# The scaled second copy of the first batch's query and key upper parts, made by ScalarE in place of VectorE

## The chip, the cores and the metric

One core of one Trainium2 chip runs the whole program. The metric is device time in microseconds (us) for one execution, and the quoted time before is the median of three runs. Engines are named as in the profile: PE is TensorE's matmul, PEld its weight load, DVE is VectorE, ACT is ScalarE, POOL is GpSimd, SP is the engine whose queue issues most transfers.

## What is computed

Three layers follow each other. The first is attention with a hash mask, over 2 batches, 8 heads, 768 positions and 64 columns; the second a gated feed-forward layer; the third a routed layer with 8 experts of which each token uses two.

```python
q_bucket = bits_to_int(einsum('bhsd,dk->bhsk', q, proj) > 0)      # the same for k
scores = where(q_bucket == k_bucket, (q @ k.T) / sqrt(64), -1e9)
x = softmax(scores) @ v                                           # 1536 x 512 after a transpose
h = x @ w_in                                                      # 512 x 2048
x = (h * sigmoid(1.702 * h)) @ w_out                              # 2048 x 512
logits = x @ w_gate + log1p(exp(x @ w_noise)) * noise             # top 2 of 8 experts per token
out[token] += weight * (relu(x @ w1[e]) @ w2[e])                  # w1[e]: 512 x 1024
```

## The kernel before

Every float32 operand of an exact matmul is split into two float16 tiles, an upper part and the rest. For a query tile (two heads, two of the six 128-row groups, so 128x256 elements) or a key tile (one head, all six groups, 128x384 elements) the function `stack_hi` does the first half of that: line L144 rounds the loaded tile to its upper part (DVE in the first batch), line L145 subtracts it from the tile on POOL, and L149 or L151 writes a second copy of the upper part, scaled by 1/32, into the tile that TensorE will read beside the rest. Which engine makes that copy is read from a table of four letters, `SC`: first batch's queries, second batch's queries, first batch's keys, second batch's keys; A is ScalarE (L149), D is VectorE (L151). In the first batch there are 12 query tiles and 8 key tiles.

`stack_lo` (L158, ACT) then writes the scaled rest into the same tile `qsa` or `ks`, and SP issues a transposing transfer of it (L169). From the transposed tile TensorE computes the hash bits (`buckets`, L179 and L180), ACT copies them out (L184), DVE makes a bucket number and a one-hot row of it (`one_hot`, L189 to L203), ACT scales it (L210), and a second transposing transfer (L211) brings it to the place from which `qk` (L254) computes masked scores. `qsa` has one buffer, `qsb` (the upper parts and one-hots of a query tile) two.

The 96 score tiles of 128 rows are numbered g = 0 to 95, 48 for each batch. For each of them DVE takes the row maximum out of PSUM (`rowmax`, L266), ACT the exponential (L275), and TensorE transposes the result (L293, with ACT copies L301) or, from the 17th tile on, it is split again (L314, L321, L323) and transposed by a transfer (L327). `pv` multiplies with the values. There are two PSUM buffers for scores, so `qk` for tile g+2 waits until `rowmax` has read tile g.

Between these steps the 32 blocks of the feed-forward weights are loaded as 64-bit words and converted: SP issues the load into a ring of three `wraw` buffers (L417), DVE turns the bits into float32 (L428, L431, L434), ACT or POOL scales (L444, L442), ACT makes the upper part (L445) and POOL the rest (L446), which frees the buffer. The feed-forward matmuls of the first 256 rows (L460, L471, with `th` on DVE in L490) begin when tile 16 and the first blocks are through.

The program names a step g for each piece of work. Up to step 99, which holds all attention work and nearly all feed-forward work, the framework's scheduler puts the instructions of each engine in order from its own estimate of their times; from step 100 the order is the written one. Each engine runs its row in order, so an instruction that waits holds all that stand behind it.

Of the kernel before, what the change touches and what calls it, by code (L numbers as in the profile page):

```python
# [53 lines left out]


PARAM = dict(GM=16, HE=lambda nm, b: 'D', OE=lambda nm, b: 'D', SC=lambda nm, b: 'D', WB=0, XO=lambda b: 'D', NG=16, WS=lambda i: 'P', TS=lambda g: True, XL=lambda g: 'D', GW=2, E0=7, T0=12, T1=16, EL=8, WX=3, PV={(1,2,3):4}, PVD=5, ST={}, VA={}, RA={}, O0=48, OS=2, IS=2, FU=16, VF=2, EC=lambda g: 'AA', QX=8, QS=3, EA=1, S1=(8,8,8,9,9,9,11,13), QE=8, XG=2, XB=2, PC=2, OH=3, BK=3, R0=18, R1=0, LK=8, WL=1, NW=3, LE=lambda nc: nc.scalar, I0=24, LQ=8, LV=0, W=[(g, 1) for g in range(-6, 30)], KA={(0,0,0):-8,(0,0,1):-6,(0,1,0):-4,(0,1,1):-2}, QA={(0,0,0):-7,(0,0,1):-3}, HI=lambda g: 'P', LO=lambda g: False)
PARAM.update(KA={(0, 0, 0): -15, (0, 0, 1): -6, (0, 1, 0): -5, (0, 1, 1): -4, (0, 2, 0): -1, (0, 2, 1): 1, (0, 3, 0): 4, (0, 3, 1): 5, (1, 0, 0): 37, (1, 0, 1): 39, (1, 1, 0): 44, (1, 1, 1): 46, (1, 2, 0): 42, (1, 2, 1): 51, (1, 3, 0): 47, (1, 3, 1): 51}, QA={(0, 0, 0): -15, (0, 0, 1): -3, (0, 0, 2): 1, (0, 0, 3): 3, (0, 1, 0): 8, (0, 1, 1): 9, (0, 1, 2): 17, (0, 1, 3): 21, (0, 2, 0): 24, (0, 2, 1): 28, (0, 2, 2): 30, (0, 2, 3): 33, (1, 0, 0): 37, (1, 0, 1): 41, (1, 0, 2): 47, (1, 0, 3): 52, (1, 1, 0): 57, (1, 1, 1): 56, (1, 1, 2): 60, (1, 1, 3): 69, (1, 2, 0): 72, (1, 2, 1): 69, (1, 2, 2): 80, (1, 2, 3): 84}, VA={(0, 0, 0): -1, (0, 0, 1): -3, (0, 1, 0): -1, (0, 1, 1): -1, (0, 2, 0): 0, (0, 2, 1): 0, (0, 3, 0): -1, (0, 3, 1): -2, (1, 0, 0): -1, (1, 0, 1): -1, (1, 1, 0): 2, (1, 1, 1): -4, (1, 2, 0): -3, (1, 2, 1): -3, (1, 3, 0): 2, (1, 3, 1): -2}, PV={(0, 0, 0): 4, (0, 0, 1): 5, (0, 0, 2): 6, (0, 0, 3): 5, (0, 1, 0): 6, (0, 1, 1): 4, (0, 1, 2): 4, (0, 1, 3): 5, (0, 2, 0): 5, (0, 2, 1): 5, (0, 2, 2): 5, (0, 2, 3): 6, (1, 0, 0): 4, (1, 0, 1): 5, (1, 0, 2): 4, (1, 0, 3): 5, (1, 1, 0): 5, (1, 1, 1): 5, (1, 1, 2): 5, (1, 1, 3): 6, (1, 2, 0): 6, (1, 2, 1): 4, (1, 2, 2): 4, (1, 2, 3): 4}, RA={0: 18, 1: 18, 2: 19, 3: 24, 4: 18}, W=[(g,1) for g in [-6, -4, -3, -1, 0, 0, 1, 1, 2, 4, 4, 7, 8, 8, 9, 10, 11, 12, 13, 14, 15, 16, 16, 17, 18, 20, 20, 22, 22, 23, 23, 24]], EC=lambda g:'AA', LE=lambda nc:nc.sync, HI=lambda g:'AAAA'[g%4], LO=lambda g:[0, 0, 0, 1, 0, 0, 0, 1][g%8]==1, S1=[8, 8, 8, 8, 8, 11, 13, 22], ST={0: 4, 1: 4, 2: 5, 3: 4, 4: 5, 5: 3}, NG=28, WS=lambda i:'PAAA'[i%4], HE=lambda nm,b:'DPDD'[2*(nm=='k')+b], OE=lambda nm,b:'DTDD'[2*(nm=='k')+b], SC=lambda nm,b:'DADD'[2*(nm=='k')+b], R1=2, I0=26, IS=1, O0=56, OS=1, GM=100, BK=3, OH=3, QX=8, QS=2, QE=7, VF=0, T0=12, T1=17, EL=10, WX=5, WL=2, PC=2, GW=2, E0=8, WB=2)
# [1094 lines left out]
```

## Time and profile before

| quantity | value |
|---|---|
| median of 3 runs | 826.06 us (823.59 to 827.40) |
| the profiled execution's own time | 823.72 us |
| its span from first to last instruction | 822.0 us |
| TensorE busy over the span | 715.9 us (87%) |
| VectorE busy | 533.9 us (65%) |
| ScalarE busy | 445.0 us (54%) |
| GpSimd busy | 267.9 us (33%) |
| mean granted TensorE clock | 0.96 |

The shares are means over a program with different stages, so a share of 65% can hide a stretch in which an engine never rests. The profiled execution took 1.72 us beside its span, and lies 2.34 us below the median.

### The profile page before, as it was taken

How to read it: one execution, taken by the hardware profiler on the slowest of the kernel's cores; microseconds unless marked ns; L12 is line 12 of the kernel's file. 1: busy time of each engine (PE TensorE's matmuls, PEld its weight loads, DVE VectorE, ACT ScalarE, POOL GpSimd, SP SyncE). 2: the span in 40 equal slices, each digit the busy share in tenths (PEclk: the TensorE clock that was granted, in tenths of full speed). 3: DMA queues.
4: the chain of work that ended last, by engine and by line, in shares of the span. 5: the costliest groups of instructions: out<-in, count | busy, mean ns of one | idle time of the engine just before them, and what ended most of it. 6: DMA issues, size and time to landing. Idle time of an engine off the chain costs nothing.

```text
span 822.0 us, 14816 instructions
## 1 busy us (share of the span) xinstructions
PE 715.9 (87%) x5398; PEld 446.0 (54%) x5399; DVE 533.9 (65%) x1330; ACT 445.0 (54%) x859; POOL 267.9 (33%) x303
## 2 busy tenths in 40 slices
...
GB/s 218 224 251 212 180 187 184 255 277 218 175 171 195 154 200 192 225 159 106 119 176 123 102 156 88 221 146 180 250 158 173 199 111 232 135 194 176 28 19 47
DMA packets 268126, 140.04 MB, mean 170 GB/s; under 512 B 224720, under 2 KB 243856, under 8 KB 268048
## 3 DMA queue, kind: packets, MB, share of 16 engines
...
## 4 chain that ended last, share of the span: by engine, by line
PE 42%; DVE 5%; DMA 3%; POOL 2%; issue 1%; ACT 1%; POOLq 0%; ACTq 0%; DVEq 0%
PE ph L799 15%; PE py L821 13%; PE px L471 6%; PE h L460 3%; PE py L825 2%; DVE er L323 1%; DMA xg<-slots 1%; PE pv L368 1%; POOL slots L685 1%; DMA slots<-xr,si 1%; DMA et<-er 1%; PE s L254 1%; ACT er L314 1%; DVE e L266 1%; DVE th L490 1%
## 5 line engine op out<-in xcount | busy, mean ns | idle before, releaser
L460 PE MATMUL h<-xt,wi 128*128 128x256 f16 x1152 | 140.2, 277 | 6.2 <-DVE mx L279 3.2
L799 PE MATMUL ph<-xg,ew 128*128 128x400 f16 (+2 forms) x864 | 135.4, 320 | 8.9 <-DMA xg<-slots 8.4
L743 DVE SCALAR_TENSOR_TENSOR ew<-w,ew 128x1024 f16<-128x1024 f32 x64 | 77.9, 1226 | 88.2 <-ACT ew L742 88.0
L471 PE MATMUL px<-wo,gt 128*128 128x512 f16 x576 | 132.6, 382 | 0.5 <-DVE th L490 0.4
L460 PEld LDWEIGHTS <-wi 128*128 128x128 f16 x1152 | 112.5, 99 | 28.2 <-issue 9.1
L821 PE MATMUL py<-ew,ht 128*128 128x512 f16 x576 | 125.8, 379 | 0.0
...
L254 PE MATMUL s<-kt,qt 128*128 128x512 f16 (+1 forms) x384 | 88.2, 353 | 33.3 <-DVE mx L266 28.5
L799 PEld LDWEIGHTS <-ew 128*128 128x128 f16 x864 | 82.6, 100 | 59.8 <-issue 6.8
L275 ACT ACTIVATE e<-e,mx 128x768 f32<-128x768 f32 x96 | 89.4, 931 | 27.9 <-DVE mx L266 21.5
L505 POOL TENSOR_TENSOR gt<-th,gt 128x512 f16<-128x512 f32 x48 | 60.1, 1252 | 122.0 <-ACT gt L504 121.6
L266 DVE CUSTOM_DVE_ANT_0 e<-s,zero 128x768 f32<-128x768 f32 x96 | 90.6, 948 | 4.4 <-PE s L254 1.5
L821 PEld LDWEIGHTS <-ht 128*128 128x128 f16 x576 | 56.3, 98 | 67.0
L471 PEld LDWEIGHTS <-gt 128*128 128x128 f16 x576 | 55.3, 98 | 64.1 <-issue 3.2
L323 DVE SCALAR_TENSOR_TENSOR er<-e,mx,er 128x768 f16<-128x768 f32 x68 | 73.1, 1080 | 25.9 <-ACT er L314 25.3
L314 ACT ACTIVATE er<-e,mx 128x768 f16<-128x768 f32 x68 | 63.0, 930 | 37.8 <-DMA et<-er 21.6
L835 ACT ACTIVATE yo<-py,wv 128x512 f32<-128x512 f32 (+1 forms) x32 | 20.3, 633 | 102.4 <-PE py L821 54.6
L809 ACT ACTIVATE ht<-ph 128x400 f16<-128x400 f32 (+2 forms) x72 | 33.5, 466 | 73.0 <-PE ph L799 72.9
L254 PEld LDWEIGHTS <-qt 128*128 128x128 f16 x384 | 37.0, 103 | 62.7 <-issue 38.5
L810 DVE SCALAR_TENSOR_TENSOR ht<-ph,ht 128x400 f16<-128x400 f32 (+2 forms) x72 | 37.6, 524 | 49.5 <-ACT ht L809 49.5
L742 ACT ACTIVATE ew<-w 128x1024 f16<-128x1024 f32 x64 | 66.3, 1047 | 2.6 <-DMA w<-in_moe_w_dram 2.6
L368 PE MATMUL pv<-et,vt 128*64 128x256 f16 x720 | 51.2, 284 | 7.5 <-DMA et<-er 7.5
...
## 6 DMA issues: line engine op xcount, KB each, us to landing
...
```

Source lines behind the costliest of these rows:

```text
L254: nc.tensor.matmul(ps[:, n0 * 128:n1 * 128], qt[:, s, h, t, :], kt[:, s, h, n0:n1, :].rearrange("p c t -> p (c t)"), start=(s == 0), stop= ...
L266: nc.vector.tensor_tensor_reduce(e32, st[g]["ps"][:, :S], zero.to_broadcast([128, S]), -0.125, TOP, op0=OP.add, op1=OP.min, accum_out=mx[: ...
L275: nc.scalar.activation(e32, e32, AF.Exp, scale=-1.0, bias=st[g]["mx"][:, 1:2], accum_out=sms[b, cc, hp][:, 2 * h + t:2 * h + t + 1] if g < ...
L314: nc.scalar.activation(er[:, 0], st[g]["e"], AF.Copy, scale=r)
L323: nc.vector.scalar_tensor_tensor(er[:, 1], d["e"], d["mx"][:, 3:4], er[:, 0], op0=OP.mult, op1=OP.subtract)
L460: nc.tensor.matmul(ph[:, a, :], wi[ws][:, d, f0:f0 + 128], xt[:, d, xs, :], start=(d == 0 and ws == 0 and xs == 0), stop=(d == HP - 1 and ...
L471: nc.tensor.matmul(px, gts[ci, f // 2][:, gs, f % 2, t * 128:t * 128 + 128], wo[ws][:, f, :], start=(f == 0 and gs == 0 and ws == 0), stop ...
L505: nc.gpsimd.tensor_tensor(gt[:, 1], th, gt[:, 0], op=OP.subtract)
L742: nc.scalar.activation(hi, x, AF.Copy, scale=SW1 if j == 0 else SW2)
L743: nc.vector.scalar_tensor_tensor(lo, x, SW1 if j == 0 else SW2, hi, op0=OP.mult, op1=OP.subtract)
L799: nc.tensor.matmul(ph[:, :c1 - c0], w[:, ws, d * FE + f * 128:d * FE + f * 128 + 128], xg[e, p][:, xs * HP + d, :], start=(d == 0 and ws = ...
L821: nc.tensor.matmul(py, ht[:, f, hs, t * 128:t * 128 + 128], w[:, ws, f * DM:(f + 1) * DM], start=(i == 0), stop=(i == n - 1))
```

## The change

Two of the four letters of `SC` become A: those of the first batch's queries and of the first batch's keys. The 12 + 8 copies of L151 in the first batch are then made by `nc.scalar.activation` in L149. Nothing else in the program text differs.

```diff
 PARAM.update(
 ...
-SC=lambda nm,b:'DADD'[2*(nm=='k')+b],
+SC=lambda nm,b:'AAAD'[2*(nm=='k')+b],
 ...
 )
```

Since the scheduler orders the instructions again, they also stand elsewhere. The first piece is DVE's row at the start of the program, where `k_131` and `q_133` are the first key and query tile as loaded and `p` is the projection:

```order
 L144 TENSOR_SCALAR ks<-k_131 128x6x64
 L144 TENSOR_SCALAR qsb<-q_133 128x4x64
-L151 TENSOR_SCALAR ks<-ks 128x6x64
-L151 TENSOR_SCALAR qsa<-qsb 128x4x64
 L97 TENSOR_SCALAR p_138<-p_135 128x6
 L98 TENSOR_TENSOR p_135<-p_135,p_138 128x6
```

DVE goes from the upper parts straight to the projection. The second piece is ACT's row at the same place:

```order
-L158 ACT_TABLE_LOAD
+L149 ACT_TABLE_LOAD
+L149 ACTIVATE ks<-ks 128x6x64
+L149 ACTIVATE qsa<-qsb 128x4x64
 L158 ACTIVATE ks<-k_131 128x6x64
 L158 ACTIVATE qsa<-q_133 128x4x64
+L149 ACTIVATE ks<-ks 128x6x64 x2
 L184 ACTIVATE pc<-pb 128x72
```

Both new copies stand ahead of both L158 rows that the first transposing transfers wait for. The third piece is DVE's row in the middle of the first batch, where `wraw_789` is the 15th of the 32 weight blocks and `e32_948` the 12th row maximum. Before:

```order
L428 TENSOR_SCALAR wf_869<-wraw_739 128x512
L194 TENSOR_REDUCE bk_1024<-pc_991 128x4
L266 ISA e32_948,mx_947<-s_880,zero_85 128x768
L266 ISA mx_947 128x1
L431 SCALAR_TENSOR_TENSOR wf_869<-wraw_739,wf_869 128x512
L203 TENSOR_TENSOR qsb_864<-iota_i_78,bk_1024 128x4x64
L434 SCALAR_TENSOR_TENSOR wraw_739<-wraw_739,wf_869 128x512
L266 ISA e32_994,mx_993<-s_942,zero_85 128x768
L266 ISA mx_993 128x1
L428 TENSOR_SCALAR wf_937<-wraw_789 128x512
L338 TENSOR_SCALAR sm_785<-sm_785 128x4
L431 SCALAR_TENSOR_TENSOR wf_937<-wraw_789,wf_937 128x512
```

And with the change:

```order
L431 SCALAR_TENSOR_TENSOR wf_869<-wraw_739,wf_869 128x512
L189 TENSOR_TENSOR pc_991<-pc_991 128x4x6
L434 SCALAR_TENSOR_TENSOR wraw_739<-wraw_739,wf_869 128x512
L191 TENSOR_TENSOR pc_991<-pc_991,pow2_89 128x4x6
L194 TENSOR_REDUCE bk_1024<-pc_991 128x4
L428 TENSOR_SCALAR wf_937<-wraw_789 128x512
L203 TENSOR_TENSOR qsb_864<-iota_i_78,bk_1024 128x4x64
L431 SCALAR_TENSOR_TENSOR wf_937<-wraw_789,wf_937 128x512
L434 SCALAR_TENSOR_TENSOR wraw_789<-wraw_789,wf_937 128x512
L266 ISA e32_948,mx_947<-s_880,zero_85 128x768
L266 ISA mx_947 128x1
```

The 15th weight block's three instructions, of which the first stood behind the 13th row maximum (`e32_994`), now stand ahead of the 12th. At the 13th row maximum DVE's row has passed two more weight blocks than before, at the 18th one more, and from the 33rd on the order of row maxima and weight blocks is the old one.

## Rows read from the trace of the kernel before

**Rows 1.** The page, parts 1 and 4: busy time by engine, the chain that ended last.
```profile
PE 715.9 (87%) x5398; PEld 446.0 (54%) x5399; DVE 533.9 (65%) x1330; ACT 445.0 (54%) x859; POOL 267.9 (33%) x303
PE 42%; DVE 5%; DMA 3%; POOL 2%; issue 1%; ACT 1%; POOLq 0%; ACTq 0%; DVEq 0%
```

**Rows 2.** Windows, stretch from:to and its length, then PE, PEld, DVE, ACT, POOL busy.
```profile
0.00:70.00 70.00, 37.18 (x302) 23.16 (x303) 65.73 (x167) 45.08 (x108) 37.06 (x73) 0.85 0.98 232
70.00:100.00 30.00, 16.14 (x110) 9.64 (x109) 22.33 (x48) 23.04 (x55) 16.81 (x17) 0.89 0.74 183
100.00:175.00 75.00, 61.19 (x495) 40.79 (x495) 72.54 (x136) 55.17 (x105) 41.73 (x35) 0.91 0.94 218
175.00:470.00 295.00, 267.77 (x2297) 179.48 (x2297) 232.72 (x667) 193.47 (x392) 94.90 (x88) 0.98 0.91 170
470.00:822.00 352.00, 333.63 (x2202) 192.94 (x2198) 140.55 (x315) 128.21 (x202) 77.44 (x92) 0.98 0.59 148
```

**Rows 3.** Waits of PE, 0 to 175 us: total us, times, longest.
```profile
PE s L254 <- DVE mx L266: 24.2, 16, 4.0
PE pb L179 <- DVE ks L144: 9.0, 1, 9.0
PE pb L179 <- DMA kt<-ks: 7.2, 3, 4.2
PE pv L352 <- DVE r L342: 6.3, 4, 3.5
PE pb L179 <- DMA qt<-qsa: 6.0, 3, 2.6
PE pb L179 <- ACT pc L184: 3.0, 1, 3.0
```

**Rows 4.** Windows of line L151 alone: DVE busy and count.
```profile
0.00:70.00 70.00, 7.22 (x14) 0.85 0.98 232
70.00:100.00 30.00, 0.91 (x2) 0.89 0.74 183
100.00:175.00 75.00, 1.62 (x3) 0.91 0.94 218
```

**Rows 5.** Line L151: duration ns, min/median/max (8 of the key rows are the second batch's).
```profile
L151 DVE TENSOR_SCALAR ks<-ks x16: 246/350/1118, 4.0 to 274.6; 128x384 f16<-128x384 f16 x16
L151 DVE TENSOR_SCALAR qsa<-qsb x12: 213/228/1177, 4.9 to 193.9; 128x256 f16<-128x256 f16 x12
```

**Rows 6.** Timeline of DVE and of POOL, 112.7 to 114.2 us: start, us, instruction.
```profile
113.00 1.18 DVE L151 TENSOR_SCALAR qsa<-qsb 128x256 f16<-128x256 f16 x1
114.10 0.94 DVE L266 CUSTOM_DVE_ANT_0 e<-s,zero 128x768 f32<-128x768 f32 x1
...
112.72 1.37 POOL L446 TENSOR_TENSOR wo<-wraw,wo 128x512 f16<-128x512 f32 x1 [1.06 <-ACT wo L445]
```

**Rows 7.** Line L149 on ACT (second batch) and line L210 on ACT, groups.
```profile
L149 ACT ACTIVATE qsa<-qsb x12: 398/416/418, 208.7 to 400.3; 128x256 f16<-128x256 f16 x12
...
L210 ACT ACTIVATE ks<-ks 128x384 f16<-128x384 f16 x8 | 4.2, 519 | 3.5 <-DVE ks L203 3.5
```

**Rows 8.** Timeline at the start, ACT and SP.
```profile
4.87 0.52 ACT L158 ACTIVATE ks<-k 128x384 f16<-128x384 f32 x1
...
5.41 1.33 SPq L169 DMA_TRANSPOSE kt<-ks  x1
```

**Rows 9.** Timeline of DVE: where the weight conversion waits for its load.
```profile
82.22 0.45 DVE L428 TENSOR_SCALAR wf<-wraw 128x512 int32<-128x512 int32 x1 [2.35 <-DMA wraw<-in_moe_w_in_dram]
90.68 0.43 DVE L428 TENSOR_SCALAR wf<-wraw 128x512 int32<-128x512 int32 x1 [2.77 <-DMA wraw<-in_moe_w_out_dram]
95.59 0.92 DVE L428 TENSOR_SCALAR wf<-wraw 128x512 int32<-128x512 int32 x1 [1.34 <-DMA wraw<-in_moe_w_out_dram]
```

**Rows 10.** Timeline of SP: first and last of five weight loads issued one after another.
```profile
86.78 0.33 SPq L417 DMA_DIRECT2D wraw<-in_moe_w_out_dram  x1
...
104.37 0.33 SPq L417 DMA_DIRECT2D wraw<-in_moe_w_out_dram  x1
```

More of the change, by code (lines that the diff above doesn't have):

```diff
@@ L56 @@
 PARAM = dict(GM=16, HE=lambda nm, b: 'D', OE=lambda nm, b: 'D', SC=lambda nm, b: 'D', WB=0, XO=lambda b: 'D', NG=16, WS=lambda i: 'P', TS=lambda g: True, XL=lambda g: 'D', GW=2, E0=7, T0=12, T1=16, EL=8, WX=3, PV={(1,2,3):4}, PVD=5, ST={}, VA={}, RA={}, O0=48, OS=2, IS=2, FU=16, VF=2, EC=lambda g: 'AA', QX=8, QS=3, EA=1, S1=(8,8,8,9,9,9,11,13), QE=8, XG=2, XB=2, PC=2, OH=3, BK=3, R0=18, R1=0, LK=8, WL=1, NW=3, LE=lambda nc: nc.scalar, I0=24, LQ=8, LV=0, W=[(g, 1) for g in range(-6, 30)], KA={(0,0,0):-8,(0,0,1):-6,(0,1,0):-4,(0,1,1):-2}, QA={(0,0,0):-7,(0,0,1):-3}, HI=lambda g: 'P', LO=lambda g: False)
-PARAM.update(KA={(0, 0, 0): -15, (0, 0, 1): -6, (0, 1, 0): -5, (0, 1, 1): -4, (0, 2, 0): -1, (0, 2, 1): 1, (0, 3, 0): 4, (0, 3, 1): 5, (1, 0, 0): 37, (1, 0, 1): 39, (1, 1, 0): 44, (1, 1, 1): 46, (1, 2, 0): 42, (1, 2, 1): 51, (1, 3, 0): 47, (1, 3, 1): 51}, QA={(0, 0, 0): -15, (0, 0, 1): -3, (0, 0, 2): 1, (0, 0, 3): 3, (0, 1, 0): 8, (0, 1, 1): 9, (0, 1, 2): 17, (0, 1, 3): 21, (0, 2, 0): 24, (0, 2, 1): 28, (0, 2, 2): 30, (0, 2, 3): 33, (1, 0, 0): 37, (1, 0, 1): 41, (1, 0, 2): 47, (1, 0, 3): 52, (1, 1, 0): 57, (1, 1, 1): 56, (1, 1, 2): 60, (1, 1, 3): 69, (1, 2, 0): 72, (1, 2, 1): 69, (1, 2, 2): 80, (1, 2, 3): 84}, VA={(0, 0, 0): -1, (0, 0, 1): -3, (0, 1, 0): -1, (0, 1, 1): -1, (0, 2, 0): 0, (0, 2, 1): 0, (0, 3, 0): -1, (0, 3, 1): -2, (1, 0, 0): -1, (1, 0, 1): -1, (1, 1, 0): 2, (1, 1, 1): -4, (1, 2, 0): -3, (1, 2, 1): -3, (1, 3, 0): 2, (1, 3, 1): -2}, PV={(0, 0, 0): 4, (0, 0, 1): 5, (0, 0, 2): 6, (0, 0, 3): 5, (0, 1, 0): 6, (0, 1, 1): 4, (0, 1, 2): 4, (0, 1, 3): 5, (0, 2, 0): 5, (0, 2, 1): 5, (0, 2, 2): 5, (0, 2, 3): 6, (1, 0, 0): 4, (1, 0, 1): 5, (1, 0, 2): 4, (1, 0, 3): 5, (1, 1, 0): 5, (1, 1, 1): 5, (1, 1, 2): 5, (1, 1, 3): 6, (1, 2, 0): 6, (1, 2, 1): 4, (1, 2, 2): 4, (1, 2, 3): 4}, RA={0: 18, 1: 18, 2: 19, 3: 24, 4: 18}, W=[(g,1) for g in [-6, -4, -3, -1, 0, 0, 1, 1, 2, 4, 4, 7, 8, 8, 9, 10, 11, 12, 13, 14, 15, 16, 16, 17, 18, 20, 20, 22, 22, 23, 23, 24]], EC=lambda g:'AA', LE=lambda nc:nc.sync, HI=lambda g:'AAAA'[g%4], LO=lambda g:[0, 0, 0, 1, 0, 0, 0, 1][g%8]==1, S1=[8, 8, 8, 8, 8, 11, 13, 22], ST={0: 4, 1: 4, 2: 5, 3: 4, 4: 5, 5: 3}, NG=28, WS=lambda i:'PAAA'[i%4], HE=lambda nm,b:'DPDD'[2*(nm=='k')+b], OE=lambda nm,b:'DTDD'[2*(nm=='k')+b], SC=lambda nm,b:'DADD'[2*(nm=='k')+b], R1=2, I0=26, IS=1, O0=56, OS=1, GM=100, BK=3, OH=3, QX=8, QS=2, QE=7, VF=0, T0=12, T1=17, EL=10, WX=5, WL=2, PC=2, GW=2, E0=8, WB=2)
```

1 line of the change is left out of this document (added).

## The prediction

> **What bounds the kernel now.** I read the page's busy shares and the chain of waits first. TensorE is busy 87% of the span and holds 42 of the hundredths that the chain names, VectorE 5 [rows 1]; so most of the program is a row of matmuls, and nothing that is done to VectorE there can pay. The change, however, touches only copies that run in the first 194 us [rows 5], so the mean shares say little and I cut the span into stretches [rows 2]. What to see: from 175 us on TensorE is busy 601 of 647 us. Before that it is not: 37.2 of 70 us, 16.1 of 30, 61.2 of 75. In the first and third of these stretches VectorE is busy 65.7 of 70 and 72.5 of 75 us; it has almost no rest, and it is the engine that sets the pace. In the one between, 70 to 100 us, no engine is full (VectorE 22.3 of 30).
>
> The waits of TensorE agree [rows 3]. Of its six longest sums up to 175 us, VectorE ends 24.2 + 9.0 + 6.3 = 39.5 us, transfers end 13.2 us, ScalarE 3.0 us. The largest is `qk` standing until a row maximum has freed a score buffer. So an item of work that leaves VectorE's row before 175 us lets row maxima and with them all matmuls come earlier, and since the order behind is unchanged and nothing there runs by a clock of its own, what is gained by 175 us should be kept to the end.
>
> **What the change removes.** Line L151 costs VectorE 7.22 us in 14 instructions up to 70 us, 0.91 us in 2 up to 100 us, and 1.62 us in 3 up to 175 us [rows 4]; the twentieth comes later. That is not what its removal is worth. Rows of VectorE overlap: one that starts at 113.00 and lasts 1.18 us ends at 114.18, and the next starts at 114.10 [rows 6]. So each gives back 0.08 us less than its duration: 14 x 0.08 = 1.1 off 7.22 leaves 6.1 us, 3 x 0.08 = 0.2 off 1.62 leaves 1.4 us. The 2 in the middle I don't count, because VectorE stands idle 7.7 us there [rows 2].
>
> Nor is all of that work. The shortest copies take 246 ns (keys) and 213 ns (queries), the longest 1118 and 1177 [rows 5]. The one at 113.00 ran beside a POOL subtraction that lasted from 112.72 to 114.09, and it ended when that ended [rows 6]. So a large part is standing behind POOL, and whether that is saved depends on what comes next in VectorE's row. If the next instruction stands in the same way, only the unhindered durations are saved: 8 x (0.246 - 0.08) + 6 x (0.213 - 0.08) = 2.1 us up to 70 us, 3 x 0.13 = 0.4 us in the third stretch. So the saving is between 2.5 and 7.5 us. What follows the copy is sometimes a row maximum, which reads PSUM and started at once at 114.10, and sometimes a weight conversion or a key's `one_hot`, from SBUF; lacking a reason for either, I take the middle, 5.0 us.
>
> The Trainium skill bears on this (SBUF — State Buffer, Who interferes with whom): VectorE and GpSimd share one pair of ports under an exclusive lock, and an instruction with two SBUF inputs contends for it too, not only a fast copy. The trace agrees for the copy (1.18 us beside POOL against 0.21 alone). By that rule alone the stall passes to the next two-input instruction, and the saving would be the lower one, 2.5 us; that is the first rival.
>
> **What it adds.** ScalarE gets 20 copies. It already makes the same query copy in the second batch, in 416 ns, and a key-sized float16 copy takes 519 ns in L210 [rows 7]: 12 x 0.416 + 8 x 0.519 = 9.1 us, against 20 unhindered ones of 12 x 0.213 + 8 x 0.246 = 4.5 us on VectorE. The work is cheaper where it was.
>
> At the start this lies on the path. The first transposing transfer is issued at 5.41 us, just as the first L158, begun at 4.87, is through [rows 8]; TensorE's first row waits for it (the 9.0 us of [rows 3]). Both new copies stand ahead of L158 in ScalarE's row (the order shows it), so the transfer goes out 0.52 + 0.42 = 0.9 us later, unless the table load hides some. I charge 0.9 us, the bounds being 0 and 0.9.
>
> Later the copies have cover: ScalarE is idle 24.9 us of the first 70 and 19.8 of the third stretch [rows 2]. In most places the copy can be made while ScalarE would stand for POOL's subtraction, since both start from L144. If the cover is gone, a copy delays an exponential or a weight's upper part behind it, and that delays TensorE's transposes or the ring of weight buffers. Bounds 0 and 9.1 us. ScalarE ends 3.0 us of TensorE's waits where VectorE ends 39.5 [rows 3], so I charge a microsecond there at 3.0 / 39.5 = 0.08 of one on VectorE: 0.7 us.
>
> **What it moves.** The scheduler puts the whole first part in a new order. Two weight blocks move ahead of the 12th and 13th row maxima (the order's third piece); at the 18th only one is still ahead, and by the 33rd none. In that stretch the weight conversion stood for its load 2.35, 2.77 and 1.34 us [rows 9], and five loads were issued from 86.78 to 104.37, so one every 17.59 / 4 = 4.40 us [rows 10]. A row maximum that stands behind two more blocks comes up to 8.8 us later at that point. But the blocks then needn't be done afterwards, and VectorE is full until 175 us; so I take zero for the move itself, with 0 and 8.8 us as bounds.
>
> **Sum.** -5.0 + 0.9 + 0.7 + 0 = -3.4 us. For the profiled execution that makes 823.72 - 3.4 = 820.3 us (span 818.6). It lay 2.34 us below the median, so against the median: 826.06 - 3.4 = 822.7 us, 0.4% less. A difference of 0.5%, 4.1 us, is about what a measurement of this kernel can tell from no change.
>
> **The rivals.**
>
> First, the stall is handed on. Then 2.5 us are saved and 1.6 paid: 826.06 - 0.9 = 825.2 us, no change. For it: weight conversions, which read two SBUF tensors, are the commonest neighbours of these copies. Against: POOL's work is not lengthened, and not every follower reads SBUF twice. Chance 0.16.
>
> Second, slower: the row maxima that now stand behind weight loads hold TensorE, and the time is not regained. The place is 70 to 100 us, the price up to 8.8 us: 822.7 + 8.8 = 831.5 us. It decides (slower by more than 4.1 us) when 7.5 of the 8.8 are kept, and it takes away the gain from 3.4 on. For it: VectorE's waits there are for transfers, which a lighter VectorE can't shorten, and ScalarE, through which each block passes twice, gets fuller. Against: TensorE stood still 13.8 us in the third stretch [rows 2], room in which to catch up. Chance 0.22; I let it stand for every loss of a reordered front.
>
> My forecast has 0.62. With the saving between 2.5 and 7.5 us and the same 1.6 paid, it runs from 826.06 - 5.9 = 820.2 to 825.2; where the two added costs vanish also, to 818.6. A second gain from the new order, which I can't price, would lie on this side as well.
>
> The Trainium skill has a rule that would speak against the change where VectorE has time (Perfetto Trace Analysis, Optimizing Scalar/DVE Operations): a copy that has a fast mode on VectorE is quicker there, and moving it pays if VectorE is saturated. Rows of this case show both halves, 0.21 against 0.42 us and 65.7 of 70 us busy, so by it the sum keeps its sign.
>
> **How the numbers follow.** The forecast's span straddles the bound of 0.5% (822.0 us): of its 0.62 I put 0.38 on faster and 0.24 on the same. The first rival gives 0.15 to the same and 0.01 to slower, the second 0.22 to slower. So faster 0.38, same 0.39, slower 0.23. The range goes from 816.0, which is the forecast's lowest end with the spread of the runs before (2.5 us below their median), to 831.5, the second rival's time.
>
> **What would show it.** In the changed profile VectorE's L151 should be gone from the first 175 us, with 20 more rows of L149 on ScalarE at 0.42 and 0.52 us. If the forecast holds, the 33rd row maximum and the first feed-forward matmul come 3 to 4 us earlier, VectorE is still above 90% up to 70 us, and from 175 us on each stretch is as long as before. If the stall is handed on, L428, L434, L189 and L203 grow by as much as L151 lost. If the second rival holds, VectorE's waits for weight loads between 60 and 110 us grow well over the 6.5 us of these three rows, and `qk` waits longer for row maxima. The first transposing transfer at 6.3 us in place of 5.41 would confirm the start's price. I would be wrong altogether if a wait of SP's queue, which serves loads and transposes in one row, moved to a worse place; the order shows its rows moved, but no row here prices that.

## The result, and the profile after

The changed kernel took 832.37 us (median of 8 runs, 830.29 to 834.99), the kernel before 824.08 us beside it (8 runs, 821.67 to 827.40). The ratio is 1.0094 with a 95% interval of 1.0077 to 1.0111, so the change costs 0.9%, about 8 us. (The ratios here and below come with their intervals and are not exactly the quotients of the two medians; here that would be 1.0101.) The forecast was 822.7 us with 816.0 to 831.5 as its range. The profiled execution took 834.11 us, its span is 832.3 us, its mean granted clock 0.96 as before.

The page of the changed kernel, parts 1 and 4, answers to [rows 1]:

```profile
PE 718.6 (86%) x5398; PEld 446.3 (54%) x5399; DVE 535.7 (64%) x1310; ACT 452.6 (54%) x879; POOL 265.6 (32%) x303
...
PE 42%; DVE 4%; DMA 3%; ACT 2%; POOL 2%; issue 1%; POOLq 0%; ACTq 0%; DVEq 0%
```

Nothing in it tells where 8 us went: VectorE has 20 instructions less, ScalarE 20 more, and TensorE's busy time is nearly as before (718.6 us for 715.9). The first three windows, which answer to [rows 2], tell more:

```profile
0.00:70.00 70.00, 35.47 (x281) 22.43 (x283) 63.29 (x149) 50.11 (x120) 38.21 (x74) 0.87 1.00 236
70.00:100.00 30.00, 20.37 (x127) 12.29 (x127) 25.02 (x49) 23.30 (x54) 16.14 (x16) 0.73 0.70 177
100.00:175.00 75.00, 58.59 (x478) 38.80 (x478) 69.42 (x125) 53.16 (x105) 41.25 (x34) 0.98 0.88 211
```

Up to 70 us VectorE (third pair of numbers) is busy 63.29 us in place of 65.73, and TensorE got less done, not more (35.47 us and 281 matmul rows for 37.18 and 302). From 100 to 175 us VectorE is busy 69.42 for 72.54, and TensorE again did less (478 matmul rows for 495; its busy time is 58.59 us at a granted clock of 0.98, for 61.19 at 0.91). Both engines rest more. Only between the two, from 70 to 100 us, did TensorE do more (127 matmul rows for 110). TensorE's four longest waits up to 175 us, which answer to [rows 3], say for what:

```profile
PE s L254 <- DVE mx L266: 25.4, 15, 5.2
PE pb L179 <- DMA kt<-ks: 16.1, 3, 9.1
PE h L460 <- ACT xt L397: 4.0, 1, 4.0
PE h L460 <- DVE th L490: 3.6, 3, 1.5
```

The wait of the start, which VectorE's L144 ended before (9.0 us), is now put down to the transfer. The feed-forward matmul L460 has two waits that were not among the six longest before, 7.6 us together.

The copies themselves went where the order said. These are line L151 in the changed kernel (all of them the second batch's keys) and L149:

```profile
L151 DVE TENSOR_SCALAR ks<-ks x8: 247/258/970, 173.1 to 283.2; 128x384 f16<-128x384 f16 x8
...
L149 ACT ACTIVATE qsa<-qsb x24: 398/412/417, 4.3 to 404.4; 128x256 f16<-128x256 f16 x24
...
L149 ACT ACTIVATE ks<-ks x8: 506/522/523, 3.8 to 46.1; 128x384 f16<-128x384 f16 x8
```

0.41 and 0.52 us each, as forecast from [rows 7]. At the start, answering to [rows 8], the timeline of ACT and SP is:

```profile
0.85 1.28 ACT L149 ACT_TABLE_LOAD   x1 [0.71 <-PEq L1139]
3.83 0.52 ACT L149 ACTIVATE ks<-ks 128x384 f16<-128x384 f16 x1 [1.70 <-DVE ks L144]
4.26 0.40 ACT L149 ACTIVATE qsa<-qsb 128x256 f16<-128x256 f16 x1
4.88 0.52 ACT L158 ACTIVATE ks<-k 128x384 f16<-128x384 f32 x1 [0.21 <-POOL k L145]
...
5.42 1.33 SPq L169 DMA_TRANSPOSE kt<-ks  x1
```

L158 begins at 4.88 (4.87 before) and the transfer goes out at 5.42 (5.41): the two copies cost nothing there, since the table load, which before stood directly ahead of L158, now begins at 0.85 and is done by 2.13. The row of before:

```profile
3.49 1.28 ACT L158 ACT_TABLE_LOAD   x1 [3.36 <-DMA k<-in_k_dram]
```

The row maxima are the best clock of this program. The start of some of them, read from VectorE's timeline, in us:

| row maximum | 9th | 13th | 17th | 25th | 29th | 30th | 31st | 33rd | 93rd |
|---|---|---|---|---|---|---|---|---|---|
| before | 65.77 | 75.23 | 99.67 | 135.10 | 154.35 | 162.56 | 167.61 | 177.22 | 445.37 |
| after | 68.93 | 86.08 | 100.70 | 139.16 | 156.09 | 171.00 | 177.42 | 184.54 | 455.03 |
| difference | +3.2 | +10.9 | +1.0 | +4.1 | +1.7 | +8.4 | +9.8 | +7.3 | +9.7 |

Two losses stand out. The first, at the 13th, is the one that the prediction priced at up to 8.8 us; it is 10.9 us, and at the 17th all but 1.0 of it has been made good. The second comes in one step, between the 29th and the 30th, and stays; 2.4 us more are lost behind the 33rd (+7.3 there, +9.7 at the 93rd).

### The profile page after: what moved, and what is told of

It is laid out like the page before. It is cut to its first block, busy times and chain, and to the rows that moved or that the text cites. A ratio compares the mean times of both kernels' runs of the same rounds, so it can differ in the third digit from the quotient of the medians.

```text
span 832.3 us, 14779 instructions
## 1 busy us (share of the span) xinstructions
PE 718.6 (86%) x5398; PEld 446.3 (54%) x5399; DVE 535.7 (64%) x1310; ACT 452.6 (54%) x879; POOL 265.6 (32%) x303
## 4 chain that ended last, share of the span: by engine, by line
PE 42%; DVE 4%; DMA 3%; ACT 2%; POOL 2%; issue 1%; POOLq 0%; ACTq 0%; DVEq 0%
PE ph L799 15%; PE py L821 13%; PE px L471 6%; PE h L460 4%; PE py L825 2%; PE pv L368 1%; DVE er L323 1%; DMA xg<-slots 1%; DMA slots<-xr,si 1%; POOL slots L685 1%; DMA et<-er 1%; PE s L254 1%; ACT er L314 1%; POOL out_dram L838 0%; DVE e L266 0%
## 5 line engine op out<-in xcount | busy, mean ns | idle before, releaser
L460 PE MATMUL h<-xt,wi 128*128 128x256 f16 x1152 | 138.8, 275 | 13.8 <-DVE th L490 6.9
L460 PEld LDWEIGHTS <-wi 128*128 128x128 f16 x1152 | 112.1, 99 | 34.9 <-issue 16.6
L505 POOL TENSOR_TENSOR gt<-th,gt 128x512 f16<-128x512 f32 x48 | 58.3, 1216 | 118.6 <-ACT gt L504 118.2
L314 ACT ACTIVATE er<-e,mx 128x768 f16<-128x768 f32 x68 | 63.0, 929 | 40.9 <-DMA et<-er 29.9
```

The source lines that it names most:

```text
L314: nc.scalar.activation(er[:, 0], st[g]["e"], AF.Copy, scale=r)
L460: nc.tensor.matmul(ph[:, a, :], wi[ws][:, d, f0:f0 + 128], xt[:, d, xs, :], start=(d == 0 and ws == 0 and xs == 0), stop=(d == HP - 1 and ...
L505: nc.gpsimd.tensor_tensor(gt[:, 1], th, gt[:, 0], op=OP.subtract)
```

## The step between the 29th and the 30th row maximum

This is the timeline of the changed kernel around it, of VectorE, POOL, ScalarE and SP:

```profile
164.65 0.43 DVE L428 TENSOR_SCALAR wf<-wraw 128x512 int32<-128x512 int32 x1 [1.99 <-DMA wraw<-in_moe_w_out_dram]
...
168.02 1.49 DVE L428 TENSOR_SCALAR wf<-wraw 128x512 int32<-128x512 int32 x1 [1.49 <-DMA wraw<-in_moe_w_out_dram]
169.55 1.53 DVE L431 SCALAR_TENSOR_TENSOR wf<-wraw,wf 128x512 int32<-128x512 int32 x1
171.00 0.94 DVE L266 CUSTOM_DVE_ANT_0 e<-s,zero 128x768 f32<-128x768 f32 x1
...
167.59 1.65 POOL L321 TENSOR_TENSOR er<-e,er 128x768 f16<-128x768 f32 x1 [3.03 <-ACT er L314]
...
166.66 0.84 ACT L314 ACTIVATE er<-e 128x768 f16<-128x768 f32 x1 [3.35 <-DMA et<-er]
...
150.35 2.63 SPq L558 DMA_DIRECT2D slots<-blank  x3
153.09 1.41 SPq L417 DMA_DIRECT2D wraw<-in_moe_w_out_dram  x1
154.61 7.16 SPq L327 DMA_TRANSPOSE et<-er  x1
```

And the same of the kernel before:

```profile
162.56 0.95 DVE L266 CUSTOM_DVE_ANT_0 e<-s,zero 128x768 f32<-128x768 f32 x1
...
157.59 1.68 POOL L321 TENSOR_TENSOR er<-e,er 128x768 f16<-128x768 f32 x1 [0.37 <-ACT er L314]
...
156.67 0.84 ACT L314 ACTIVATE er<-e 128x768 f16<-128x768 f32 x1 [0.68 <-DMA et<-er]
...
149.49 2.89 SPq L327 DMA_TRANSPOSE et<-er  x1
```

Two holds are seen here (a hold is a row in which an engine stands, and with it all that is behind), and each by itself would keep the 30th row maximum well behind its old time. The first is on VectorE. The 30th and part of the 31st weight block stand ahead of the row maximum; VectorE waits 1.99 and 1.49 us for their loads, and the last of these rows ends just as the row maximum begins. Counted at L434, the last row of a block, VectorE has passed 2, 3, 2 and 1 blocks more than before at the 30th, 31st, 32nd and 33rd row maximum, and as many from the 34th on; so the old order does not come back at the 33rd, and between the 18th and the 33rd it is further off than at the 18th. The second hold is a chain from SP over ScalarE to POOL. On POOL, L321 of tile 27 (numbered from 0, the 28th) ends at 169.24; `e32` has two buffers, so the 30th row maximum can't write before that. L321 waits for ScalarE's L314, which waits 3.35 us for a transposing transfer, because `er` has two buffers too and tile 25 has not left the first. SP issues that transposing transfer from 154.61 to 161.77, behind three `slots<-blank` transfers of 1032 KB each and a weight load; its data had been ready at 151.59 (end of VectorE's L321 of that tile). Before, the first of the `slots` transfers stood alone and the transfer was through at 152.38.

## Experiments

In most of them the order of each engine's row is written out. The function below links each instruction to the one that is to stand ahead of it on its engine, without a wait between them; ORDER lists the instructions.

```diff
+            pin(tc, nc)
             order.enter_context(tc.manual_schedule(engines={
...
+def pin(tc, nc):
...
+        if i.engine in last:
+            tc.add_manual_dep(i, last[i.engine].name, mybir.DependencyInfo(
+                mybir.DependencyClass.NoSync, mybir.DependencyReason.DATA), reason="pin")
+        last[i.engine] = i
```

"Old order" means the rows of the kernel before on all five engines, "new order" those of the changed kernel.

**The engine or the order.** The first has `SC` as 'AAAD' and the old order, the second `SC` as 'DADD' and the new order.

> The 20 copies on ScalarE, but every engine runs the order of before (the 20 copies stand in ScalarE's row where the old order would issue them). If the new order is what costs (theory O), the time is that of before or a little less: 820 to 825 us, since VectorE is lighter by up to 7 us up to the 33rd row maximum. If the copies on ScalarE cost by themselves (theory C: they hold exponentials and weight parts up), it is as slow as the change: 829 to 834 us. In either case, if the stall behind POOL is handed on, VectorE's other rows up to the 33rd row maximum grow by most of the 5 us that L151 stood above its unhindered duration.

> The copies on VectorE as before, but every engine runs the order of the changed kernel. Theory O: as slow as the changed kernel or slower, 831 to 838 us, with the 33rd row maximum 7 us late. Theory C: the time of before, 822 to 826 us.

Measured: copies on ScalarE in the old order 824.50 us beside 824.76 of before, ratio 1.0008 (0.9985 to 1.0031). Copies on VectorE in the new order 834.42 us, ratio 1.0135 (1.0098 to 1.0172). So theory O holds and theory C falls: the order alone makes the kernel slower (its 33rd row maximum comes at 188.72, 11.5 us late where 7 were expected), and the exchange of engines alone changes nothing that can be measured. Whether the exchange gains something in the new order stays open: 1.0094 with it and 1.0135 without, with intervals that overlap.

That the exchange gains nothing needs a reason too, since VectorE has less to do. The windows up to the 17th row maximum and from there to the 33rd, of the kernel before, of the old order with ScalarE's copies and of the changed kernel:

```profile
0.00:99.67 99.67, 53.33 (x410) 32.80 (x412) 87.73 (x213) 67.82 (x160) 53.54 (x90) 0.86 0.91 218
99.67:177.22 77.55, 63.41 (x505) 41.80 (x505) 75.09 (x141) 57.41 (x109) 43.08 (x36) 0.91 0.95 218
```
```profile
0.00:100.15 100.15, 53.46 (x410) 33.27 (x412) 81.69 (x198) 73.39 (x176) 51.70 (x89) 0.84 0.94 216
100.15:178.50 78.35, 66.66 (x506) 43.49 (x506) 76.79 (x139) 58.30 (x112) 43.91 (x37) 0.87 0.95 216
```
```profile
0.00:100.70 100.70, 56.39 (x410) 35.11 (x412) 89.01 (x198) 74.11 (x175) 54.86 (x91) 0.83 0.91 219
100.70:184.54 83.84, 63.53 (x517) 41.58 (x517) 77.42 (x143) 59.58 (x117) 46.57 (x38) 0.96 0.85 209
```

In the old order VectorE's busy time up to the 17th row maximum fell from 87.73 to 81.69, by 6.0 us, and the 17th came at 100.15 in place of 99.67. All of the 6.0 us became rest. What the rest went into is seen in the waits up to the 17th row maximum, TensorE's before, then TensorE's and VectorE's in the old order with ScalarE's copies:

```profile
PE s L254 <- DVE mx L266: 13.7, 10, 3.3
PE pb L179 <- DMA kt<-ks: 7.2, 3, 4.2
```
```profile
PE pb L179 <- DMA kt<-ks: 20.0, 4, 9.1
PE s L254 <- DVE mx L266: 10.0, 9, 1.8
```
```profile
DVE wf L428 <- DMA wraw<-in_moe_w_out_dram: 5.8, 2, 3.8
DVE wf L428 <- DMA wraw<-in_moe_w_in_dram: 3.8, 4, 1.2
```

TensorE waits 3.7 us less for row maxima. For the keys' transposing transfers it waits 20.0 us, 9.1 of them the wait of the start, which was put down to L144 before; the other 10.9 are 3.7 more than the 7.2 of before. VectorE waits 9.6 us for weight loads, before 6.8. So what VectorE gave back is found again as waits in front of transfers. The DMA share of this stretch (last but one number of the windows) is 0.91 and 0.94. Whether these transfers come late because the DMA engines are full, or because ScalarE, on which they depend, is now busier (73.39 us for 67.82), no run separates. In the stretch behind it the changed kernel takes 5.5 us more than the old order; its VectorE is busy 0.6 us more and rests 6.42 us in place of 1.56. So the loss is waiting of VectorE, not work.

**One letter at a time.** 'AADD' and 'DAAD', each in the order that the scheduler makes for it.

```diff
-SC=lambda nm,b:'DADD'[2*(nm=='k')+b],
+SC=lambda nm,b:'AADD'[2*(nm=='k')+b],
```

> Only the 12 query copies go to ScalarE; the scheduler makes an order of its own, a third one. Theory O: any time from 820 to 836 us, not bound to lie between before and after. Theory C: ScalarE gets 12 of the 20 copies (5.0 of 9.1 us), so about half of the loss, 826 to 829 us.

> Only the 8 key copies go to ScalarE, all in the first 50 us; a fourth order. Theory O: any time from 820 to 836 us. Theory C: 8 of the 20 copies (4.2 of 9.1 us), 826 to 829 us, and the first batch's row maxima are late already at 50 us.

Measured: queries alone 830.21 us (1.0062, 1.0036 to 1.0089), keys alone 825.68 us (1.0022, 1.0000 to 1.0044). The smaller copies cost more, which no price of a copy explains; each letter gives an order of its own. With the keys alone the 33rd row maximum is at 186.51, 9.3 us late, but the 93rd at 444.79, as early as before. So a loss at the 33rd can be regained in another order of what follows.

**Which half of the order.** Copies on ScalarE; the new order up to the 17th row maximum and the old for what is left, the reverse, and the old order up to the 25th, then the new.

> Copies on ScalarE; new order up to the issue of the 17th row maximum (about 100 us), the order of before for all that is left then. If the first front (weight blocks ahead of the 9th to 13th row maxima, +10.85 us at the 13th) costs the time: 830 to 832. If that is regained, as the +1.0 at the 17th says, and the second part of the order is the cost: 822 to 826.

> The other half: order of before up to the issue of the 17th row maximum, the new order for the rest. If the second part is the cost: 830 to 833, with the 31st row maximum 8 to 10 us late as in the changed kernel. If the first part is: 823 to 826.

> Copies on ScalarE; order of before up to the issue of the 25th row maximum (135 us), then the new order. If the loss of the changed kernel lies in the piece with the last four weight blocks (they stand ahead of the 30th and 31st row maxima in the new order): 829 to 834, with the 31st row maximum 5 to 10 us later than the 25th. If it lies between the 17th and the 25th: 824 to 827.

| kernel | time, us | ratio (interval) | 17th | 25th | 30th | 33rd | 93rd |
|---|---|---|---|---|---|---|---|
| old order throughout | 824.50 | 1.0008 (0.9985 to 1.0031) | 100.15 | 135.29 | 163.72 | 178.50 | 446.35 |
| new to 17th, then old | 827.02 | 1.0028 (1.0004 to 1.0051) | 102.19 | 137.71 | 165.44 | 179.68 | 444.95 |
| old to 17th, then new | 839.16 | 1.0192 (1.0163 to 1.0221) | 98.42 | 142.74 | 174.70 | 188.25 | 455.18 |
| old to 25th, then new | 833.30 | 1.0092 (1.0071 to 1.0113) | 99.66 | 134.16 | 170.73 | 184.27 | 455.06 |

The time of the first of these runs lies between its two expected ranges, that of the second above both. The order up to 100 us costs little: 1.0028, with an interval that just leaves out 1. The part behind the 25th row maximum is enough for the whole 0.9%. The halves don't add up: the new second half behind the old first one is worse than the new order throughout, so how much the piece from the 17th to the 25th costs by itself is not shown, and no run has the old order up to the 33rd and the new one behind it.

**Single moves on SP.** In the first, the new order has the three `slots<-blank` transfers behind the last weight load; in the second, the old order has them together ahead of the 30th load. In the third, eight weight loads of the new order go ahead of the transfers behind which they had stood; in the fourth, five loads of the old order go behind one or two rows more. The first as an example, in SP's row:

```diff
 L417 DMA wraw<-in_moe_w_out_dram
-L558 DMA slots<-blank x3
-L417 DMA wraw<-in_moe_w_out_dram
-L327 DMA_TRANSPOSE et<-er
 L417 DMA wraw<-in_moe_w_out_dram x2
-L327 DMA_TRANSPOSE et<-er x2
+L327 DMA_TRANSPOSE et<-er
+L417 DMA wraw<-in_moe_w_out_dram x2
+L558 DMA slots<-blank
+L327 DMA_TRANSPOSE et<-er
+L558 DMA slots<-blank
```

> The changed kernel in the new order on every engine; only the first three slots<-blank transfers (L558), which the new order issues together ahead of the 30th weight load, are issued one by one behind the 32nd. Theory S (those three transfers, 2.63 us each just ahead of the loads that VectorE then stands for, make the lasting loss at the 31st row maximum, which came 9.8 us later than before): VectorE's L428 waits at 164 and 168 us vanish, the 33rd row maximum comes 3 to 7 us earlier than the 184.5 of the changed kernel, the time falls to 826 to 829. Theory T (the loads' place among the transposing transfers Te and the row maxima queued behind three weight blocks make it, not the slots): no more than 1.5 us, 831 to 833.

> Copies on ScalarE in the order of before (which took 824.5), with one thing moved: the first three slots<-blank transfers are issued together ahead of the 30th weight load, as in the new order. Theory S: VectorE's L428 stands for the 30th to 32nd loads, the 33rd row maximum 3 to 7 us later, time 827 to 831. Theory T: 824 to 826.

> The changed kernel in its new order on PE, VectorE, ScalarE and POOL; on SP's queue alone, eight weight loads (the 20th, 22nd to 24th, 27th and 29th to 31st) that went out 1 to 5 us after their buffer was free are put ahead of the transposing transfers or query loads that they stood behind. Theory Q (a wait of SP's queue: loads stand behind transposes, so VectorE stands for loads): L428's waits for wraw between 100 and 185 us fall from 7 to under 2 us, the 33rd row maximum comes 4 to 8 us earlier than 184.5, the time is 824 to 829. Theory V (VectorE's row is the cause: three weight blocks are due there before the ring of three buffers can be filled again, whatever SP does): the waits move to the ring or to the transposes, the time stays at 830 to 834.

> Copies on ScalarE in the order of before (824.5); on SP's queue five weight loads (the 20th, 23rd, 24th, 29th and 30th) are put later by the one or two rows by which the new order has them late. Theory Q: VectorE begins to stand for loads, the 33rd row maximum is 2 to 6 us later than 178.5, the time 827 to 831. Theory V: 823 to 826.

Measured: 832.04 us (1.0093, 1.0064 to 1.0123), 826.32 (1.0017, 0.9991 to 1.0044), 837.57 (1.0157, 1.0138 to 1.0176) and 826.23 (1.0004, 0.9986 to 1.0022). So theories S and Q both fell: neither the `slots` transfers nor late loads make the loss by themselves, and earlier loads make it worse, by 5.2 us against the changed kernel, more than theory V allowed too. (The 2.63 us that theory S gives to each of the three `slots` transfers are the issue of all three.) With the loads early, VectorE's waits for them from 100 to 185 us are gone (5.1 us in the changed kernel), and yet its 33rd row maximum comes at 190.92. ScalarE's waits from 100 us on show why. L314's wait for a transposing transfer, first in the changed kernel (to 190 us), then with loads early (to 190 us), then in the old order (to 180 us):

```profile
ACT er L314 <- DMA et<-er: 9.9, 7, 3.3
```
```profile
ACT er L314 <- DMA et<-er: 14.0, 6, 3.6
```
```profile
ACT er L314 <- DMA et<-er: 4.2, 5, 1.3
```

A load that stands early in SP's row waits there for POOL to free its `wraw` buffer, and the transposing transfers wait behind it. SP's own waits for that from 100 to 185 us, in the changed kernel and with loads early:

```profile
SPq L417 <- POOL wo L446: 2.2, 4, 0.8
```
```profile
SPq L417 <- POOL wo L446: 24.0, 8, 5.2
```

**Single moves on VectorE.** In the new order the 30th row maximum goes ahead of the five weight rows; in the old order, the reverse; in the third, eight row maxima of the old order go ahead of one to three weight rows each. The second as an example:

```diff
+L434 wraw<-wraw,wf
+L428 wf<-wraw
+L431 wf<-wraw,wf
+L434 wraw<-wraw,wf
+L428 wf<-wraw
+L431 wf<-wraw,wf
 L266 e_1977,mx<-s,zero
...
-L434 wraw<-wraw,wf
...
```

> The changed kernel in its new order, with one row of one engine moved: on VectorE the 30th row maximum stands ahead of the five weight rows (L428, L431, L434 of the 30th block, L428 and L431 of the 31st) behind which the new order put it and in which VectorE stood 1.99 and 1.49 us for loads. Theory V (row maxima held behind weight blocks between the 17th and the 33rd cost the time): the 30th row maximum comes at 162 to 164 in place of 171.0, the 33rd 2 to 6 us earlier than 184.5, the time 826 to 830.5. Theory W (the row maximum only waits where something else would make it wait: the pace there is set by ScalarE's and the transfers' work): 33rd within 1.5 us, 831 to 833.

> Copies on ScalarE in the order of before (824.5), with the reverse edit: on VectorE the last row of the 29th weight block, the 30th block and the first two rows of the 31st are put ahead of the 30th row maximum, all else in the order of before. Theory V: the 30th row maximum 6 to 10 us later than 163.7, the 33rd 3 to 8 us later than 178.5, 828 to 832. Theory W: 33rd within 2 us, 823 to 826.

> Copies on ScalarE in the order of before, with eight row maxima between the 9th and the 32nd put ahead of the one to three weight rows that stood directly ahead of them on VectorE. Theory V: the 33rd row maximum 1 to 3 us earlier than 178.5, 821 to 824, faster than both kernels. Theory W: 824 to 826.

Measured: 833.76 us (1.0097, 1.0078 to 1.0116), 829.77 (1.0048, 1.0031 to 1.0065) and 827.17 (1.0022, 1.0000 to 1.0045). Taken out of the new order, the hold on VectorE gives nothing; the row maximum, alone now, waits for the next one. Its row with the weight rows behind it:

```profile
171.11 0.96 DVE L266 CUSTOM_DVE_ANT_0 e<-s,zero 128x768 f32<-128x768 f32 x1 [6.63 <-POOL er L321]
```

Put into the old order, the same hold costs 4.4 us (829.77 against 825.38 of before beside it; by the ratio's interval 2.6 to 5.4 us). The 30th row maximum comes at 170.77, the 33rd at 182.20, the 93rd at 451.56, that is 7.1, 3.7 and 5.2 us later than in the old order, and TensorE's waits from 100 to 180 us show it in one of 8.6 us:

```profile
PE s L254 <- DVE mx L266: 13.5, 3, 8.6
```

Row maxima put further ahead gain nothing (827.17, above the ranges of both theories); theory V holds for this one place, not as a rule.

**Transposing transfers early and late.** In the new order the transfers of tiles 25 to 27 go ahead of the last loads; in the old order those of tiles 25 and 26 go behind the 29th and 30th load; then the first with the 30th row maximum ahead as well; last, this with the query's transposes early and all `slots` transfers late. The second:

```diff
-L327 DMA_TRANSPOSE et<-er
-L417 DMA wraw<-in_moe_w_out_dram
-L327 DMA_TRANSPOSE et<-er
-L417 DMA wraw<-in_moe_w_out_dram
+L417 DMA wraw<-in_moe_w_out_dram x2
+L327 DMA_TRANSPOSE et<-er x2
```

> The changed kernel in its new order; on SP's queue alone the transposing transfers of tiles 25, 26 and 27 (et<-er, L327) are put ahead of the last three weight loads, in the sequence load 28, transpose 25, load 29, transpose 26, load 30, transpose 27, load 31, and the three slots transfers behind them. Theory X (in the new order those transposes stand 10.2 and 12.1 us behind slots transfers and weight loads in SP's row; that keeps the two er buffers, so ScalarE's L314 of tile 27 stands 3.35 us for a transfer, POOL's L321 frees an exponential's buffer only at 169.24, and the 30th row maximum waits for that, at 171.0 against 162.6 before): L314 of tile 27 at 156 to 160 in place of 166.66, the 30th row maximum at 164 to 168 (the 30th and 31st weight blocks stand ahead of it still), the 33rd 3 to 7 us earlier than 184.5, time 825 to 829.5. Theory Y (SP's place is a result and not the cause): 831 to 834.

> Copies on ScalarE in the order of before (824.5); on SP's queue alone the transposing transfers of tiles 25 and 26 are put behind the loads of weight blocks 28 and 29. Theory X: transpose 25 goes out some 10 us after its tile is ready (4.1 in the order of before), L314 of tile 27 is 4 to 8 us later than 157.5, the 33rd row maximum 3 to 6 us later than 178.5, time 827 to 831. Theory Y: 823 to 826.

> As the kernel with transposes 25 to 27 early, and on VectorE the 30th row maximum ahead of the five weight rows, which alone gained nothing since it then waited 6.63 us for POOL's L321. Theory X: both holds are gone, the 30th row maximum at 162 to 164, the 33rd within 2 us of 178.5, time 823 to 827. Theory Y: 831 to 834.

> The new order with the 30th row maximum ahead of the five weight rows on VectorE, and SP's rows from the 29th weight load on in the sequence load 28, transpose 25, query transpose (L169), load 29, transpose 26, load 30, query transpose (L211), transpose 27, load 31, transposes 28 and 29, and each slots transfer behind a later transpose. Theory X (holds through SP's single row make the loss at the 30th to 33rd row maximum; when the transposes of tiles went first, the slots transfers stood ahead of the query's transposes, and VectorE's L144 stood 5.9 us with the 31st row maximum behind it): without that hold the 31st row maximum comes at 169 to 174, the 33rd at 178 to 183, time 824 to 829. Theory Y (PE's or ScalarE's place in the new order makes it, whatever SP does): the 33rd at 184 or later, 831 or more.

| kernel | time, us | ratio (interval) | 29th | 30th | 31st | 33rd |
|---|---|---|---|---|---|---|
| transfers early, new order | 834.39 | 1.0115 (1.0083 to 1.0147) | 155.87 | 168.77 | 183.39 | 190.49 |
| transfers late, old order | 828.44 | 1.0038 (1.0016 to 1.0060) | 152.92 | 166.01 | 170.49 | 180.23 |
| transfers and row maximum early, new order | 835.27 | 1.0126 (1.0098 to 1.0154) | 154.79 | 164.89 | 182.10 | 189.20 |
| query's transposes early too, `slots` late | 840.09 | 1.0176 (1.0153 to 1.0199) | 157.99 | 168.48 | 179.24 | 186.35 |

The late transfers in the old order go the way of theory X, though less far: SP issues them at 155.64, behind a load that waits for its buffer, L314 of tile 27 stands 7.24 us for one and comes 3.6 us late (4 to 8 expected), the 33rd row maximum 1.7 us (3 to 6). They cost 4.0 us by the medians (828.44 against 824.49), 1.3 to 4.9 us by the ratio's interval; that of the old order without this move, 0.9985 to 1.0031, overlaps with it, so the cost is less certain than that of the weight rows.

```profile
148.86 6.73 SPq L417 DMA_DIRECT2D wraw<-in_moe_w_out_dram  x2
155.64 4.88 SPq L327 DMA_TRANSPOSE et<-er  x2
...
161.09 0.84 ACT L314 ACTIVATE er<-e 128x768 f16<-128x768 f32 x1 [7.24 <-DMA et<-er]
```

In the new order, on the other hand, the time from the 29th to the 30th row maximum, 14.91 us after and 8.21 before, shrinks to 13.21 with the row maximum ahead, 12.90 with the transfers early and 10.10 with both. That is 4.8 of the 6.7 us of the step, and still nothing of the time comes back: the 31st is then held. With the transfers early, the three `slots` transfers stand ahead of the query's transposes, and VectorE's L144 waits for one of these with the row maximum behind it:

```profile
169.41 3.31 SPq L558 DMA_DIRECT2D slots<-blank  x3
172.77 3.70 SPq L211 DMA_TRANSPOSE qt<-qsb  x1
...
183.18 0.29 DVE L144 TENSOR_SCALAR qsb<-q 128x256 f16<-128x256 f32 x1 [5.93 <-DMA qt<-qsb]
```

The last kernel has this hold off too, and its 33rd row maximum is still at 186.35; then the `slots` transfers, now late, stand among the transposing transfers of tiles 32 to 34, which SP begins 3.3, 5.0 and 10.6 us after their data are ready (3.1, 0.0 and 1.0 us in the changed kernel), and the kernel ends slowest of all. Theory X names a hold that is there, and is wrong that it is all of it.

In the six kernels with the new order and one or more holds off, VectorE's longest wait behind the 17th row maximum is one that VectorE does not show in the changed kernel. With the `slots` late, the loads early, the transfers early, and the transfers and the row maximum early it is L144 for the query's transposing transfer (5.4, 5.2, 5.9 and 6.2 us); with the row maximum early alone and in the last kernel it is the row maximum for POOL's L321 (6.6 and 3.5 us).

No run has one engine alone in the new order beside four in the old, so the engines are not told apart in that way.

## Why the prediction was wrong

**What bounds the kernel.** It said that VectorE, with almost no rest up to 70 us, sets the pace, and that what leaves its row lets row maxima come earlier. This step failed. In the old order 6.0 us left its row and the row maxima came no earlier (the 17th at 100.15 for 99.67, the 33rd at 178.50 for 177.22); TensorE's and VectorE's waits moved to transfers. [rows 3] already held a warning: of the 39.5 us put down to VectorE, 9.0 are the wait of the start, which, as the prediction says itself further on, ends with the first transposing transfer; it is still there in the changed kernel. And [rows 2] held a second full resource that the reading passed over: the DMA share of 0.98 up to 70 us and 0.94 from 100 to 175 us. That the DMA engines are what binds there is a reading; no run here took load off them. The prediction also put the Trainium skill (Perfetto Trace Analysis, Optimizing Scalar/DVE Operations) more strongly than it stands: the page says of work on a saturated VectorE that offloading some of it "may make sense", not that it pays. Here VectorE was busy 65.7 of 70 us, and it was worth 0.

**What the change removes.** The term was -5.0 us with 2.5 to 7.5 as bounds. As busy time of VectorE it measured 6.0 us up to the 17th row maximum and 4.3 up to the 33rd (162.82 to 158.48 us, the sums of the windows above); as time of the kernel it measured 0, between -1.2 and +2.6 (the interval of 1.0008 times 824.76), together with the two added terms. Its lower bound should have been nothing.

**What it adds.** The start, 0.9 us, is 0: the lower bound that the text gave, since the table load stood before where the two copies stand now (in the old order with the copies on ScalarE the first transfer goes out at 5.65, 0.2 us late). ScalarE's later copies, 0.7 us, can't be told from 0 in the sum above.

**What it moves.** This is the term that decided. It was taken as 0 with 8.8 us as its upper bound, and measured 832.37 - 824.50 = 7.9 us (7.1 by the two ratios), or with the copies on VectorE 834.42 - 824.76 = 9.7 us. So the step that failed is this zero: a new order of the rows was priced at nothing, and it was the whole loss. The reason given, that blocks done early needn't be done later, was right at the place it spoke of: the 10.9 us at the 13th row maximum shrank to 1.0 at the 17th, and the kernel with the new order up to there takes 827.02. The error was to stop reading the order at 100 us, and to take "by the 33rd none" as a sign that nothing between could cost: at the 30th to 32nd row maximum the same order has 2, 3 and 2 blocks more ahead, more than at the 18th.

**The rivals.** The first, a stall handed on, would have given 0.9 us less than before; the old order with ScalarE's copies comes to 824.50 beside 824.76. Part of it is the stall handed on. Up to the 33rd row maximum L151 is gone with 9.9 us, and all other rows of VectorE together last 3.6 us longer: L431 takes 28.5 us in 31 instructions for 25.3 in as many before. The sign that the prediction named is not seen, though: L428, L434, L189 and L203 take 62.5 us together for 62.6. And VectorE's rest grew as well, and that rival had no place for it. The second gave 831.5 us with a chance of 0.22 and stood for every loss of a reordered front. It has the sign and nearly the size. That it came near is luck: its place, 70 to 100 us, is wrong, its sign failed (VectorE's waits for loads between 60 and 110 us are 4.3 us, against 6.8 before), and so did its mechanism. Loads did keep VectorE waiting, 10.5 us up to 175 us against 6.8, but the old order with ScalarE's copies has 9.6 us of such waits and loses nothing, and removing single waits gave nothing back.

**What would make it wrong altogether** was named last: a wait of SP's queue that moves to a worse place. There is one, the transposing transfer of tile 25 behind `slots` transfers and a load. Such a wait, put alone into the old order, costs 4.0 us by the medians, and the weight rows ahead of one row maximum cost 4.4. Shown is that the order costs the 8 us, that its part from the 25th row maximum on is enough for it, and that it holds two things of which one costs 2.6 to 5.4 us alone and the other 1.3 to 4.9. Not shown is which rows would have to go back for the whole of it: six kernels that took one or more holds out of the new order gained nothing. Still open is also an order that beats both kernels. The keys alone on ScalarE lost 9.3 us up to the 33rd row maximum and had them back by the 93rd, so an old first part with that later part might gain; no run has it.
